# Padded value rows in DRAM, and keys, block rows and first weights requested later

## The chip, the cores and the metric

The kernel runs on one core of a Trainium2 chip. The metric is the device time of one execution in microseconds (us). Runs of this kernel before the change took 737.98, 738.64 and 740.18 us, median 738.64.

## The reference

Two parts follow each other. The first is an attention over 4 batches, 8 heads, 768 positions and head size 64. Each position sees its neighbours less than 16 away, and beside them 24 block summaries: of each block of 32 positions, the maximum of its keys and the mean of its values.

```python
k_sum = k.reshape(B, H, nb, block, D).max(axis=3)
v_sum = v.reshape(B, H, nb, block, D).mean(axis=3)
scores_l = scale * np.matmul(q, k.transpose(0, 1, 3, 2))        # masked to |i - j| < 16
scores_s = scale * np.einsum('bhsd,bhnd->bhsn', q, k_sum) + np.log(block)
a = softmax(concatenate([scores_l, scores_s]))
attn = np.matmul(a, concatenate([v, v_sum], axis=2))
```

The second is a mixture of 8 experts on the 3072 rows of the result (512 wide). A gate picks two experts for each row by noisy logits; each expert computes relu(x @ w1) @ w2 with a hidden size of 1024; the two results are added with softmax weights. All inputs are 32 bit.

## The kernel before, in words

**The attention** is cut into 24 steps of 128 queries, six to a batch. A step has two windows of 64 queries; for each, 94 keys and values and the 24 summaries make the 118 columns of its scores. The work of a step is spread over several turns of one loop over t: the turn computes the scores of step t + 2 (`scores`, L304), their row maximum on VectorE (`smax`, L311), transposes the probabilities of step t + 1 (L324), exponentiates those of step t + 2 on ScalarE (L318), multiplies the probabilities of step t with its values (`av`, L337, 32 matmuls), and normalizes step t - 1 (`norm`, L346 to L355). After that come the gate's own matmul (L378), for which the row is transposed (L366), and a store of the row, split into two 16-bit halves, to DRAM (`x_out`, L361, tile `xr` to `xd`).

**What the change touches** is how inputs reach the core. All plain loads are issued by the sync engine (SP), one after the other, and a load that must wait for its buffer holds up what is queued behind it.

- Keys (`load_k`, L102): two buffers `kb`, one for even and one for odd batches, each filled in halves of 384 positions. A margin of zero columns lies left and right of the keys; `kx_local` (L113) copies each window out of the buffer, and `k_piece` (L221) takes the block maxima on VectorE.
- Values of windows (`v_window`, L268, tile `vw`): for each window 96 rows of 520 numbers (8 heads, 64 values and a 1). A step's windows are asked for two steps ahead, when the buffers have been read. For batches 1 to 3 the first four windows also get the block sums (`v_rest`, L275).
- Block rows (`load_vb`, L135, landing in `htl`, `hth` and once in `stg`): the 32 values of a block of a head as one row, 96 rows at a time, in two halves of 16 values. VectorE adds the halves (`v_sum`, L229), GpSimd the rest (`v_sum2`, L234), and the sums are stored to DRAM (`v_sum_out`, L263) and read back by `v_rest`. Batch 0 has its sums from matmuls on tiles of 128 rows (`load_vn`, L140).
- Weights of expert 0, first half (`w_load`, L579, tile `stg`): four slices, each split into two 16-bit parts on ScalarE (`w_hi`, L587) and VectorE (`w_lo`, L596, `w1l`).

When each of these is placed is written out by hand: `at(t, f, ...)` puts a call into turn t of the loop, and the part behind the point says where in the turn (.5 ahead of `smax`, .1 to .3 ahead of `av`, .8 at the turn's end; a whole number just behind `av`, ahead of the turn's window loads). The lists W0 and WC place loads and splits of the weights, KL and KP loads and maxima of the keys (relative to the batch's six steps), VL loads and VS sums of the block rows.

Gates of whole groups of steps are worked out in the same way (`gate_a` to `gate_u`, from L398 on), most of it in small VectorE instructions; group 0 has the steps 0 to 4, group 1 the steps 5 to 9, group 2 the steps 10 to 12.

**The experts** follow. For each, rows are gathered by the gate's tables, transposed by DMA, and pass through the two products (`mm1`, L650, and `mm2`, L696 and L692), while the next expert's weights are loaded and split.

Of the kernel before, what the change touches and what calls it, by code (L numbers as in the profile page):

```python
# [17 lines left out]
B, H, S, D = 4, 8, 768, 64  # L18
BLK, WIN = 32, 16
NB = S // BLK  # L20
P = 128
# [8 lines left out]
W = 64 + 2 * (WIN - 1)  # L30
NK = W + NB
PAD = WIN - 1
KW = S + 2 * PAD + 2
VR = 96
VP = S + VR - 64
H0, CAP = 384, 816
# [4 lines left out]
CL = 1  # L41
SK = HP * NK
SW = 16 * (D + 1)
NCH = 7
R = 4096
RC = R // P
NS = 8 * NCH
GN = 5
# [10 lines left out]
def attn_moe(ctx, tc, qt, kt, vt, vb, wgn, noise, w1, w2, out):  # L59
    nc = tc.nc  # L60
# [27 lines left out]

    LAST = NCH - 1
    NL = CAP - LAST * P  # L90
    HWD = CAP + 64 - NL
    HT = [moe.tile([P, FC, HWD], F16, name=x) for x in ("hth", "htl")]
    KB, VW, KX = [], [], []
    for i in range(2):
        KB.append(keep.tile([P, HP, KW], F32, name=f"kb{i}"))
    for i in range(QN):
# [2 lines left out]
    QR = {}  # L99

    def load_k(b, j, n=1):
        nc.sync.dma_start(KB[b % 2][:, :, PAD + j * P:PAD + (j + n) * P], kt[b, :, :, j * P:(j + n) * P])  # L102

    def load_q(t):
        QR[t] = QT[t % QBUF]
# [2 lines left out]

    def kx_local(t):
        b, j = divmod(t, TS)  # L110
        k = KB[b % 2][:, :, j * P:j * P + 64 + W]
        for blk in range(2):
            (nc.vector if t < 2 else nc.gpsimd).tensor_copy(KX[t % QN][:, :, blk, NB:NK],  # L113
                                                            k[:, :, 64 * blk:64 * blk + W])
# [7 lines left out]
    def q_piece(t):  # L122
        kx_local(t)
        kx_sum(t)

    VB = {}

    def load_vb(u, i):
        n = 2 * u + i
        if n == 7:  # L130
            VB[u, i] = stage.tile([P, SW], F32, name="stg")
        else:
            n = n - 1 if n < 7 else (n - 8) % 6
            VB[u, i] = HT[n // 3].rearrange("p f n -> p (f n)").bitcast(F32)[:, SW * (n % 3):SW * (n % 3 + 1)]
        nc.sync.dma_start(VB[u, i][:96], vb[u * 96:(u + 1) * 96, SW * i:SW * i + SW])  # L135

    VN = [HT[0].rearrange("p f n -> p (f n)").bitcast(F32)[:, H * (D + 1) * j:H * (D + 1) * (j + 1)] for j in range(TS)]

    def load_vn(j):
        nc.sync.dma_start(VN[j].rearrange("p (h d) -> p h d", h=H), vt[0, PAD + j * P:PAD + (j + 1) * P])  # L140

    load_q(0)
    for j in range(0, TS, 2):
        load_k(0, j, 2)


    ji = HT[1].rearrange("p f n -> p (f n)").bitcast(I32)[:, SW:SW + P]
    nc.gpsimd.iota(ji, pattern=[[1, P]], base=0, channel_multiplier=-1)
# [10 lines left out]

    spare = [x.rearrange("p f n -> p (f n)").bitcast(F32)[:, 3 * SW:] for x in HT]  # L160
    dist, dist2 = [spare[1][:, W * i:W * i + W] for i in range(2)]
# [5 lines left out]
    for i in range(3):  # L167
# [8 lines left out]
                   allow_small_or_imprecise_dtypes=True)  # L176
    ind0 = HT[1].rearrange("p f n -> p (f n)").bitcast(F32)[:, 2 * SW:2 * SW + TS * NB].rearrange("p (t n) -> p t n", t=TS)
    nc.vector.tensor_scalar(ind0, ind, float(-BLK), None, op0=OP.is_gt)
# [8 lines left out]
    nc.gpsimd.iota(iotar, pattern=[[1, P]], base=0, channel_multiplier=0, allow_small_or_imprecise_dtypes=True)  # L187
    iotac = const.tile([P, E, NCH], F16, name="iotac")
    nc.gpsimd.iota(iotac, pattern=[[RC, E], [1, NCH]], base=0, channel_multiplier=0,
                   allow_small_or_imprecise_dtypes=True)  # L190
# [5 lines left out]
    wg32 = const.tile([P, DC, 16], F32, name="wg32")  # L196

    for x in KB:
        nc.gpsimd.memset(x[:, :, 0:PAD], 0.0)
        nc.gpsimd.memset(x[:, :, PAD + S:], 0.0)  # L200
    for i in range(8):
        VW.append(keep.tile([P, H, D + 1], F32, name=f"vw{i}"))
    late = []
# [1 line left out]
    for i in range(4):  # L205
        x = moe.tile([P, 2 * DM], F16, name=f"xg{i}")
# [10 lines left out]
    def k_piece(b, j, n=1):  # L217
        if j == 0:
            KM[b] = work.tile([P, HP, NB], F32, name="kmax")
        src = KB[b % 2][:, :, PAD + j * P:PAD + (j + n) * P]  # L220
        nc.vector.tensor_reduce(KM[b][:, :, 4 * j:4 * (j + n)],  # L221
                                src.rearrange("p h (n i) -> p h n i", i=BLK), axis=AX.X, op=OP.max)

# [41 lines left out]
    def v_window(blk):  # L265
        b, j = divmod(blk, 2 * TS)
        x = VW[(b % 2) * 4 + j % 4]
        nc.sync.dma_start(x[NB:NB + VR], vt[b, 64 * j:64 * j + VR])  # L268
        if j < 4 and b:
            v_rest(blk)  # L270
        return x

    def v_rest(blk):
        b, j = divmod(blk, 2 * TS)
        nc.sync.dma_start(VW[(b % 2) * 4 + j % 4][0:NB], vsd[b].rearrange("h n d -> n h d"))  # L275
# [3 lines left out]
    def v_load(t):  # L279
        VX[t] = [v_window(2 * t), v_window(2 * t + 1)]  # L280
# [180 lines left out]
    TB0 = const.tile([P, 3, 2], I32, name="tb0")  # L461
    TB = const.tile([P, E, NCH, 2], I32, name="tb")

# [105 lines left out]
    def w_alloc(e):  # L569
        pool = late[0] if e % 2 else wpool  # L570
        WT[e] = {n: pool.tile([P, 4, 1024], F16, name=f"{n}{e % 2}") for n in ("w1h", "w1l", "w2h", "w2l")}
# [50 lines left out]
    def x_gather(e, c, rows=N):  # L622
        if c == 0:
            XTE[e] = (late[0] if e % 2 else moe).tile([P, 2 * DC, CAP], F16, name="xte")
        n = min(P, CAP - c * P)
        x = XG[gi[0] % len(XG)]
        gi[0] += 1
        r = indirect(
            out=x[:n], out_offset=None, in_=xd[:rows],
            in_offset=bass.IndirectOffsetOnAxis(ap=tb_of(e, c)[:n, 0:1], axis=0),  # L630
            bounds_check=rows - 1, oob_is_err=False)
        XC[e, c] = x
        return r
# [87 lines left out]
    def at(t, f, *a):  # L721
        todo.setdefault(round(t, 3), []).append((f, a))
# [13 lines left out]
    for j in range(TS):  # L736
        load_vn(j)
# [4 lines left out]
    for j in range(4):  # L742
        k_piece(0, j)
    kx_local(0)
    for j in range(4, TS):
        k_piece(0, j)
# [3 lines left out]
    at(-0.8, v_first_out)  # L750

    w_alloc(0)
    W0 = [7, 11, 15, 18]
    WC = [10, 14, 17, 21]
    for i in range(4):
        at(W0[i], w_load, 0, i)
        at(WC[i] + 0.8, w_hi, 0, i)
        at(WC[i] + 1.8, w_lo, 0, i)
    VS = [(2, 3), (6, 7), (12, 14)]
    KP = [-3, -3, -2, -1, 1, 2]  # L760
    KP0 = [0, 1, 1, 2, 2, 2]
    KL = [-6, -6, -6, -3, -3, -3]
    VL = [(0, 1), (2, 2), (8, 9)]
    for b in range(B - 1):
        for j in range(TS):
            at(6 * b + KP[j] + 0.5 if b else KP0[j] + 0.5, k_piece, b + 1, j)
            if j % 3 == 0:
                at(6 * b + KL[j] if b else -1 + j // 3, load_k, b + 1, j, 3)
        for h in range(2):
            y = VS[b][h]  # L770
            for i in range(2):
                at(VL[b][h], load_vb, 2 * b + 2 + h, i)
            at(y + 0.5, v_sum, 2 * b + 2 + h)
            at(y + 0.1, v_sum2, 2 * b + 2 + h)
            at(y + 1, v_sum_out, 2 * b + 2 + h)
# [30 lines left out]
    for t in range(-2, NT):  # L806
        if t + QA < NT:
            load_q(t + QA)
        u = t + 3
# [22 lines left out]
        if u < NT and t >= 1:  # L832
            kx_local(u)
# [22 lines left out]
    for i in range(3):  # L856
        x = late[0].tile([P, DM], F32, name=f"prev{i}")
# [66 lines left out]
    assert not todo, todo  # L924
    for c in range(3, NCH):
        x_gather(0, c)
# [4 lines left out]
    k = 0  # L931
# [107 lines left out]
def layout(q, k, v, moe_w_gate, moe_w_noise, moe_noise, moe_w1, moe_w2):  # L1039
    import numpy as np  # L1040

    c = np.ascontiguousarray

    def heads(x):
        return c(x.reshape(B, HP, 2, S, D).transpose(0, 2, 4, 1, 3).reshape(B, 2 * D, HP, S))

    v1 = np.concatenate([v, np.ones((B, H, S, 1), v.dtype)], axis=3)
    vp = np.zeros((B, VP, H, D + 1), v.dtype)
    vp[:, PAD:PAD + S] = v1.transpose(0, 2, 1, 3)
    wgn = np.concatenate([moe_w_gate, moe_w_noise], axis=1).reshape(DC, P, 2 * E).transpose(1, 0, 2)  # L1050
    return {
        "qt": c(heads(q).reshape(B, 2 * D, HP, TS, P).transpose(0, 3, 1, 2, 4).reshape(B, TS, 2 * D, HP * P)),
        "kt": heads(k), "vt": vp,
        "vb": v1.reshape(B * H * NB, BLK * (D + 1)), "wgn": c(wgn),
        "noise": c(moe_noise.reshape(NT, P, E).transpose(1, 0, 2)), "w1": c(moe_w1), "w2": c(moe_w2),
    }

# [15 lines left out]
```

## Time and profile before

| | |
|---|---|
| median of three runs | 738.64 us |
| profiled execution | 741.86 us |
| its span, first to last instruction | 740.1 us |
| mean granted TensorE clock in it | 0.963 |
| TensorE busy | 694.0 us |
| VectorE busy | 323.2 us |
| ScalarE busy | 234.8 us |
| GpSimd busy | 283.1 us |
| moved by DMA | 126.21 MB |

The span is 1.8 us shorter than the time of the same execution; the rest lies around it. A row of the page that shows the span in 40 slices has one digit for each 18.5 us. The chain of waits gives a start, a length and what the time was spent on; a piece that begins with DMA is a wait for that transfer. A row of a stretch of time gives the stretch, its length, the busy time of the engines in the order TensorE, its weight load, VectorE, ScalarE, GpSimd with the number of instructions, the granted clock, the busy share of the 16 DMA engines and the rate in GB/s; asked for one line, only engines that run it appear. A row of waits gives the total, the count and the longest.

### The profile page before, as it was taken

Reading aid. Unit: us, or ns where it says so; the run is one execution under the profiler, and the core shown is the slowest. Engines: PE = TensorE matmul, PEld = TensorE weight load, DVE = VectorE, ACT = ScalarE, POOL = GpSimd, SP = SyncE. Lnnn points to the kernel's source line nnn. Section 1 sums busy time; section 2 is a strip of 40 time slices with the busy share of each in tenths; the row PEclk is TensorE's granted clock in tenths of the full one; section 3 lists DMA queues with packets and bytes.
Section 4 is the critical chain, followed back from the end, with each engine's and each line's share of the span. In section 5 each row is a group of like instructions: output and inputs, shape, how many; then the busy total and the mean of one; then the engine's idle time right before and its main releaser. Section 6 shows DMA issues by size and latency. Waiting matters only on the chain.

```text
span 740.1 us, 13612 instructions
## 1 busy us (share of the span) xinstructions
PE 694.0 (94%) x5330; PEld 409.2 (55%) x5330; DVE 323.2 (44%) x686; ACT 234.8 (32%) x523; POOL 283.1 (38%) x464
## 2 busy tenths in 40 slices
PE   7979897887989999999999999999999999999992
PEld 6667686765535555455446545554654555455441
DVE  6647868685934344234414431541353143412210
ACT  3568766771404044024203310430242033102100
POOL 2566556443040550553234243414432342340141
PEclk9999988985999999999999999999999999999997
DMA  9998987273269698569826941993497289511020
GB/s 284 283 281 249 278 230 215 92 186 122 88 156 364 207 276 195 151 179 222 235 84 162 198 169 65 192 224 131 112 214 180 86 169 163 159 47 38 23 80 33
DMA packets 105418, 126.21 MB, mean 171 GB/s; under 512 B 63701, under 2 KB 68445, under 8 KB 105344
## 3 DMA queue, kind: packets, MB, share of 16 engines
q1 hardware_dynamic: 93200, 88.96, 48.0%
q0 software_dynamic: 12144, 36.28, 18.1%
q8 instruction: 44, 0.72, 0.5%
q14 instruction: 30, 0.25, 0.1%
HBM read 88.14 MB, written 26.36 MB: 155 GB/s over the span
## 4 chain that ended last, share of the span: by engine, by line
PE 73%; DMA 11%; DVE 9%; SPq 1%; ACT 1%; POOL 1%; issue 1%; POOLq 0%; DVEq 0%
PE h L650 32%; PE pt L696 29%; PE pt L692 3%; DMA vw<-in_vt_dram 2%; PE o L337 2%; DMA htl<-in_vb_dram 2%; PE s L304 2%; DMA stg<-in_vb_dram 2%; PE pt L324 1%; PE o L378 1%; DMA stg<-in_w_dram 1%; DMA xd<-xr 1%; DMA xg<-xd,tb 1%; DVE w1l L596 1%; DVE w2l L596 1%
## 5 line engine op out<-in xcount | busy, mean ns | idle before, releaser
L650 PE MATMUL h<-xte,w1h 128*128 128x432 f16 (+1 forms) x1024 | 201.9, 338 | 3.6 <-DVE htl L655 2.9
L654 ACT ACTIVATE hth<-h 128x432 f16<-128x432 f32 (+1 forms) x128 | 63.7, 507 | 287.9 <-PE h L650 284.7
L86 POOL DMA_INDIRECT out_dram<-y,tb x48 | 53.4, 1113 | 244.7 <-DVE y L703 214.0
L650 PEld LDWEIGHTS <-w1h 128*128 128x128 f16 x1024 | 99.9, 98 | 81.1 <-issue 7.2
L696 PEld LDWEIGHTS <-hth 128*128 128x128 f16 x768 | 75.1, 98 | 91.8 <-issue 2.3
L655 DVE SCALAR_TENSOR_TENSOR htl<-h,hth 128x432 f16<-128x432 f32 (+1 forms) x128 | 73.2, 580 | 96.2 <-ACT hth L654 94.5
L650 PE MATMUL h<-xte,w1l 128*128 128x432 f16 (+1 forms) x512 | 109.9, 338 | 0.0
L703 DVE SCALAR_TENSOR_TENSOR y<-pt,tb,prev 128x512 f32<-128x512 f32 x42 | 31.5, 750 | 149.2 <-PE pt L696 149.2
L86 POOL DMA_INDIRECT xg<-xd,tb x56 | 58.9, 1052 | 95.9 <-DMA xte<-xg 59.7
L696 PE MATMUL pt<-w2l,hth 128*128 128x512 f16 x384 | 91.0, 379 | 1.5 <-DVE w2l L596 1.5
L696 PE MATMUL pt<-w2h,htl 128*128 128x512 f16 x384 | 90.7, 379 | 0.0
L696 PE MATMUL pt<-w2h,hth 128*128 128x512 f16 x384 | 90.7, 379 | 0.0
L650 PEld LDWEIGHTS <-w1l 128*128 128x128 f16 x512 | 50.3, 98 | 38.8 <-issue 0.9
L587 ACT ACTIVATE w2h<-stg 128x1024 f16<-128x1024 f32 x32 | 33.8, 1055 | 92.4 <-DMA stg<-in_w_dram 92.4
L696 PEld LDWEIGHTS <-htl 128*128 128x128 f16 x384 | 37.6, 98 | 45.3
L596 DVE SCALAR_TENSOR_TENSOR w2l<-stg,w2h 128x1024 f16<-128x1024 f32 x32 | 39.1, 1222 | 52.5 <-ACT w2h L587 51.8
L86 POOL DMA_INDIRECT prev<-out_dram,tb x42 | 46.9, 1116 | 10.9 <-issue 10.9
L318 ACT ACTIVATE p<-s,nm 128x118 f32<-128x118 f32 x192 | 50.5, 375 | 0.8
L358 POOL TENSOR_TENSOR xr<-x,xr 128x512 f16<-128x512 f32 x24 | 30.3, 1261 | 50.6 <-ACT xr L355 43.3
L596 DVE SCALAR_TENSOR_TENSOR w1l<-stg,w1h 128x1024 f16<-128x1024 f32 x32 | 41.7, 1302 | 15.3 <-ACT w1h L587 12.3
L337 PE MATMUL o<-vw,pts 118*64 118x65 f32 x768 | 34.9, 247 | 5.7 <-DMA vw<-in_vt_dram 5.6
L337 PEld LDWEIGHTS o<-vw,pts 118*64 118x64 f32 x768 | 30.3, 158 | 11.8 <-DMA vw<-in_vt_dram 8.3
(164 smaller groups left out, 641.9 us busy)
## 6 DMA issues: line engine op xcount, KB each, us to landing
stg<-in_w_dram SPq DMA_DIRECT2D x64, 512.0 KB
vw<-in_vt_dram SPq DMA_DIRECT2D x48, 195.0 KB
q<-in_qt_dram SPq DMA_DIRECT2D x24, 256.0 KB
xd<-xr SPq DMA_DIRECT2D x24, 256.0 KB
kb<-in_kt_dram SPq DMA_DIRECT2D x6, 768.0 KB
out_dram<-prev SPq DMA_DIRECT2D x6, 768.0 KB
htl<-in_vb_dram SPq DMA_DIRECT2D x6, 390.0 KB
hth<-in_vb_dram SPq DMA_DIRECT2D x5, 390.0 KB
```

Source lines behind the costliest of these rows:

```text
L86: return nc.gpsimd.indirect_dma_start(**kw)
L318: nc.scalar.activation(PE_[t][:, a, hp, :], SC[t][:, a, hp, :], AF.Exp, bias=NM[t][:, 1, a, hp:hp + 1], scale=0.125)
L337: nc.tensor.matmul(o[64 * blk:64 * blk + 64, h // 4, c:c + D + 1], PT[t][:NK, h % 2, h // 2, 64 * blk:64 * blk + 64], VX[t][blk][:NK, h, : ...
L358: nc.gpsimd.tensor_tensor(XR[t][:, DM:], X[t], XR[t][:, 0:DM], op=OP.subtract)
L587: nc.scalar.activation(WT[e][n + "h"][:, i % 4, :], SG[e, i], AF.Copy, scale=sc)
L596: nc.vector.scalar_tensor_tensor(lo, SG[e, i], sc, hi, op0=OP.mult, op1=OP.subtract)
L650: nc.tensor.matmul(ph[:, :n], w[wn][:, c, f * P:(f + 1) * P], x[:, xo + c, c0:c1], start=(k == 0), stop=(k == 11))
L654: nc.scalar.activation(hh[:, f, c0:c1], ph[:, :n], AF.Relu)
L655: nc.vector.scalar_tensor_tensor(hl[:, f, c0:c1], ph[:, :n], 0.0, hh[:, f, c0:c1], op0=OP.max, op1=OP.subtract)
L692: nc.tensor.matmul(py[64 * i:64 * i + 64, :HD], hx[:, f, c * P:c * P + 64], wv[:, f, HD * i:HD * i + HD], start=(k == 0), stop=(k == 23), ...
L696: nc.tensor.matmul(py, hx[:, f, c * P:c * P + P], wv[:, f, :], start=(k == 0), stop=(k == 23))
L703: nc.vector.scalar_tensor_tensor(y, py[:, :d], gw, pv[:, :d], op0=OP.mult, op1=OP.add)
```

## The change

Three things change.

1. In DRAM, the rows of the values (520 numbers, 2080 bytes) are padded to 576 numbers (2304 bytes), and the half rows of the block rows (1040 numbers, 4160 bytes) to 1088 (4352 bytes), so that each starts on a multiple of 256 bytes. The loads take the same numbers as before. The layout of the inputs is made ahead of the kernel.
2. The margin of the key buffer is 16 columns on each side; it was 15 on the left and 17 on the right. `kx_local` starts one column further right to read the same keys.
3. Requests move. Keys of batches 2 and 3: first half from six to three steps ahead of the batch before them, second half from three to one; the first four maxima come one step later too. Block rows of batch 2 from steps 2 and 2 to 4 and 5, those of batch 3 from 8 and 9 to 10 and 12. Weight slices from steps 7, 11, 15, 18 to 12, 14, 16, 18, their splits from 10, 14, 17, 21 to 15, 17, 19, 21. (A batch's block rows and keys are numbered by the batch that reads them.)

```diff
-KW = S + 2 * PAD + 2
+KO = 16
+KW = S + 2 * KO
+VC = H * (D + 1)
+VROW = 576
+VBROW = 1088
...
-        k = KB[b % 2][:, :, j * P:j * P + 64 + W]
+        k = KB[b % 2][:, :, KO - PAD + j * P:KO - PAD + j * P + 64 + W]
...
-        nc.sync.dma_start(VB[u, i][:96], vb[u * 96:(u + 1) * 96, SW * i:SW * i + SW])
+        nc.sync.dma_start(VB[u, i][:96], vb[u * 96:(u + 1) * 96, i, :SW])
...
-        nc.sync.dma_start(VN[j].rearrange("p (h d) -> p h d", h=H), vt[0, PAD + j * P:PAD + (j + 1) * P])
+        nc.sync.dma_start(VN[j], vt[0, PAD + j * P:PAD + (j + 1) * P, :VC])
...
-        nc.sync.dma_start(x[NB:NB + VR], vt[b, 64 * j:64 * j + VR])
+        nc.sync.dma_start(x[NB:NB + VR].rearrange("p h d -> p (h d)"), vt[b, 64 * j:64 * j + VR, :VC])
...
-    W0 = [7, 11, 15, 18]
-    WC = [10, 14, 17, 21]
+    W0 = [12, 14, 16, 18]
+    WC = [15, 17, 19, 21]
...
-    KP = [-3, -3, -2, -1, 1, 2]
+    KP = [-2, -2, -1, 0, 1, 2]
...
-    KL = [-6, -6, -6, -3, -3, -3]
-    VL = [(0, 1), (2, 2), (8, 9)]
+    KL = [-3, -3, -3, -1, -1, -1]
+    VL = [(0, 1), (4, 5), (10, 12)]
...
-    vp = np.zeros((B, VP, H, D + 1), v.dtype)
-    vp[:, PAD:PAD + S] = v1.transpose(0, 2, 1, 3)
+    vp = np.zeros((B, VP, VROW), v.dtype)
+    vp[:, PAD:PAD + S, :VC] = v1.transpose(0, 2, 1, 3).reshape(B, S, VC)
+    vb = np.zeros((B * H * NB, 2, VBROW), v.dtype)
+    vb[:, :, :SW] = v1.reshape(B * H * NB, 2, SW)
```

More of the change, by code (lines that the diff above doesn't have):

```diff
@@ L101, in load_k @@
     def load_k(b, j, n=1):
-        nc.sync.dma_start(KB[b % 2][:, :, PAD + j * P:PAD + (j + n) * P], kt[b, :, :, j * P:(j + n) * P])
+        nc.sync.dma_start(KB[b % 2][:, :, KO + j * P:KO + (j + n) * P], kt[b, :, :, j * P:(j + n) * P])
     def load_q(t):
@@ L198, in attn_moe @@
     for x in KB:
-        nc.gpsimd.memset(x[:, :, 0:PAD], 0.0)
-        nc.gpsimd.memset(x[:, :, PAD + S:], 0.0)
+        nc.gpsimd.memset(x[:, :, 0:KO], 0.0)
+        nc.gpsimd.memset(x[:, :, KO + S:], 0.0)
     for i in range(8):
@@ L219, in k_piece @@
             KM[b] = work.tile([P, HP, NB], F32, name="kmax")
-        src = KB[b % 2][:, :, PAD + j * P:PAD + (j + n) * P]
+        src = KB[b % 2][:, :, KO + j * P:KO + (j + n) * P]
         nc.vector.tensor_reduce(KM[b][:, :, 4 * j:4 * (j + n)],
@@ L1053, in layout @@
         "kt": heads(k), "vt": vp,
-        "vb": v1.reshape(B * H * NB, BLK * (D + 1)), "wgn": c(wgn),
+        "vb": vb, "wgn": c(wgn),
         "noise": c(moe_noise.reshape(NT, P, E).transpose(1, 0, 2)), "w1": c(moe_w1), "w2": c(moe_w2),
```

## The prediction, made before the changed kernel ran

> **What bounds the kernel now.** I read the slices of the page first (18.5 us each), then the chain that ended last, then one line's work in single stretches of time.
>
> ```profile
> PE   7979897887989999999999999999999999999992
> PEclk9999988985999999999999999999999999999997
> DMA  9998987273269698569826941993497289511020
> ```
>
> Up to 111 us (six slices) the 16 DMA engines are at least eight tenths busy and TensorE is not full. From the seventh slice the DMA engines have room, and from about 222 us TensorE is full to the end. The change moves transfers of the first six slices, so it is priced there. The chain says who is waited for:
>
> ```profile
> 27.33 11.89 DMA stg<-in_vb_dram
> 39.29 8.55 DMA htl<-in_vb_dram
> 47.90 7.58 DMA vw<-in_vt_dram
> ...
> 63.54 1.33 DVE hth L229
> ...
> 66.14 7.54 DMA xd<-xr
> 73.69 4.48 DMA htl<-in_vb_dram
> ...
> 82.37 9.71 DMA vw<-in_vt_dram
> 92.12 2.46 PE o L337 x32
> ...
> 100.05 1.08 PE o L337 x32
> ...
> 109.77 1.08 PE o L337 x32
> ...
> 119.90 2.53 DVE w1l L596
> ...
> 127.88 1.67 PE o L337 x32
> ```
>
> Six DMA pieces, 49.8 us together, stand in it between 27 and 92 us; after that come TensorE and VectorE. A step of the attention ends with the 32 matmuls of L337, so these rows are a clock for the steps: 100.05 is step 12 (counted from 0), 109.77 step 14, 127.88 step 16. Undisturbed, a step takes (109.77 - 100.05) / 2 = 4.86 us. The slow stretch:
>
> ```profile
> 28.90:99.80 70.90, 16.85 (x352) 14.22 (x352) 0.93 0.99 267
> ...
> 28.90:99.80 70.90, 61.80 (x964) 50.15 (x962) 49.30 (x116) 49.65 (x150) 46.96 (x64) 0.93 0.99 267
> ```
>
> In the first row, of L337 alone, 352 matmuls are 11 steps (1 to 11): 70.9 us, where 11 x 4.86 = 53.5 would do. The excess of 17.4 us is what this change can touch. In the second row TensorE is busy for 61.8 of it, so 9.1 us is plain idling; the rest is slower work, partly at a lower granted clock (0.93 here): after the wait that ends at 92.12, L337 takes 2.46 us, not 1.08. A wait removed takes such a tail with it.
>
> **Part 1: the padding.** It removes no byte and no transfer; each row of V windows (2080 B) and block rows (4160 B) now starts on a multiple of 256 B. It pays only if the starts are what makes these transfers slow. They are slow:
>
> ```profile
> 8.00:13.00 5.00, 2.78 (x58) 1.93 (x59) 4.32 (x11) 0.00 (x0) 0.94 (x2) 1.00 1.06 391
> 14.00:18.00 4.00, 4.00 (x31) 2.36 (x24) 1.14 (x1) 3.90 (x15) 0.00 (x0) 0.69 1.05 251
> 20.00:24.00 4.00, 4.00 (x50) 2.31 (x48) 1.95 (x4) 0.00 (x0) 1.19 (x3) 1.00 1.04 367
> 34.00:38.00 4.00, 3.46 (x70) 2.54 (x70) 3.05 (x6) 1.98 (x9) 3.84 (x5) 1.00 1.03 237
> ```
>
> ```profile
> 4.59 5.40 SPq L140 DMA_DIRECT2D hth<-in_vt_dram  x6
> 10.33 2.73 SPq L268 DMA_DIRECT2D vw<-in_vt_dram  x4
> ...
> 34.70 3.37 SPq L135 DMA_DIRECT2D hth<-in_vb_dram  x3
> ```
>
> The last column of the stretches is GB/s; the other rows are issues of the sync engine. The six L140 tiles, queued ahead of the windows, pass in the first stretch: rows of the same tensor, of the same 2080 B, at the same odd starts, but 128 rows each, and they run at 391 GB/s. Windows of 96 rows from that tensor follow (14 to 18: 251), block rows, again 96 rows, dominate the last (237). What separates 391 from 251 is the number of rows a transfer has, not where its rows start, so I take the padding's gain as 0; the other end is that all 96-row transfers rise to 367 (rival 1). Below nothing: a row pitch 11% wider (2304 for 2080) could slow reading by at most that 11%, 0.1 us per window of 195 KB.
>
> The Trainium skill (DMA: Bandwidth & Descriptors, "How a descriptor splits into AXI transactions") says a transfer that starts off a 256 B boundary also fetches the bytes from the boundary on; an estimate from it is 65 beats for an aligned 2080 B row and 68.5 on average now, 5% of each window. The 391 GB/s of the unaligned L140 rows shows no such 5%. The Trainium skill (SBUF — State Buffer, "Door 1: The DMA port swizzle") speaks against any gain: partitions 0 to 63 share eight of 16 ports, so 96 rows from 0 fill some ports twice as full as others, whatever the source's pitch; by it the block rows reach 391 x 96/128 = 293 GB/s at best, an estimate that lies on the same side as the 237.
>
> **Part 2: transfers asked for later.** Sizes and places:
>
> ```profile
> vw<-in_vt_dram SPq DMA_DIRECT2D x48, 195.0 KB
> kb<-in_kt_dram SPq DMA_DIRECT2D x6, 768.0 KB
> htl<-in_vb_dram SPq DMA_DIRECT2D x6, 390.0 KB
> stg<-in_w_dram SPq DMA_DIRECT2D x64, 512.0 KB
> q<-in_qt_dram SPq DMA_DIRECT2D x24, 256.0 KB
> xd<-xr SPq DMA_DIRECT2D x24, 256.0 KB
> ```
>
> ```profile
> 79.27 0.55 SPq L102 DMA_DIRECT2D kb<-in_kt_dram  x1
> 79.92 1.06 SPq L135 DMA_DIRECT2D hth<-in_vb_dram  x2
> 82.37 1.04 SPq L268 DMA_DIRECT2D vw<-in_vt_dram  x2
> ```
>
> The windows of step 11 are the 82.37 issue, and they landed at 92.1 because of what stood ahead in the same queue. Of that, the change puts behind them: one half of batch 3's keys (step 9 to 11; 786 kB at 367 GB/s = 2.1 us), four block-row loads (steps 8 and 9 to 10 and 12; 4 x 399 kB at 237 = 6.7 us) and one weight slice (step 7 to 12; 524 kB at 367 = 1.4 us). That is 10.2 us of queue time gone from before step 11. Within the stretch the rest is spread: batch 2's block rows go from one burst of four at step 2 (6.7 us) to two at step 4 and two at step 5, its keys from steps 0 and 3 to 3 and 5. A step's own transfers (two windows at 237, q and xd of 262 kB each at 367) take 1.7 + 1.4 = 3.1 us of 4.86, so a burst of four delays the next windows, and a pair (3.4 us) fits in two steps. I therefore expect the waits on windows to nearly vanish up to step 11, and TensorE to set the pace.
>
> What comes in their place, of the 17.4 us:
> - VectorE. The gate of the first batch ran under the 9.71 us wait and now stands in the open. The second batch's shows the price: steps 15 and 16 take 18.1 us (109.77 to 127.88), 8.4 over the pace, of which 2.5 is the weight split w1l at 119.90. Between 0 and the other 5.9, part of it a lower clock, I take the middle, 3 us. Four block sums of 1.33 us (L229, in the chain at 63.54) on steps that also reduce keys: 5.3 at most, 0 if idle time takes them; 2 us.
> - Keys. The key maximum (L221) sits in VectorE's order ahead of the scores' maximum; behind it wait exp, transposes and the next step. Its pieces come 1.5 steps (7.3 us) after their load, where there were 2.5 to 3.5. For batch 2's second half, issued behind two block-row loads, a window pair and q and xd (3.4 + 1.7 + 1.4 us, plus its own 2.1 = 8.6), the load ends 1.3 us too late, and I take 3 us with the clock's tail, which at 92.12 was 1.4 us on L337 alone. The other three are behind less: 0.
>
> ```profile
> DVE kmax L221 <- DMA kb<-in_kt_dram: 4.5, 3, 2.4
> SPq L102 <- POOL kx L113: 4.7, 1, 4.7
> ```
>
> Today's waits there are 4.5 us in all, longest 2.4: the lower end of that price is 0, the upper 4.6 a load (rival 3). The second row is a gain: SP stood 4.7 us in front of a key load whose buffer was still read, windows and q behind it; asked for three steps later, it finds the buffer free. At step 3 it stands behind the block-sum store (L263) in SP's order, as the second half did; what waits behind it (windows, q) waits no longer than now.
>
> So 17.4 - 3 - 2 - 3 = 9.4 us come out by step 12.
>
> **After step 12.** Block rows and a weight slice at step 12 (3.4 + 1.4 us on top of 3.1) make two steps' traffic in one: 1.5 us late once, between 0 (the seventh slice has room) and 4.8. The weight splits: the second moves from 15.8 to 18.8 in steps, away from the gate, and the third from 18.8 to 20.8.
>
> ```profile
> 119.82 2.61 DVE L596 SCALAR_TENSOR_TENSOR w1l<-stg,w1h 128x1024 f16<-128x1024 f32 x1
> ...
> 129.60 0.17 DVE L346 TENSOR_SCALAR r<-o 128x8 f32<-128x8 f32 x1 [2.27 <-PE o L337]
> ...
> 141.64 1.22 DVE L596 SCALAR_TENSOR_TENSOR w1l<-stg,w1h 128x1024 f16<-128x1024 f32 x1
> ...
> 155.20 0.15 DVE L346 TENSOR_SCALAR r<-o 128x8 f32<-128x8 f32 x1
> ```
>
> The 2.5 us at 119.9 leave the chain. The first split now falls into the 2.27 us in which VectorE idled before 129.60: 0. The third falls right ahead of 155.20, where VectorE had no idle time: 1.2 us. Net 1.3 gained. The other edits (16 columns of margin for 15, reads of keys shifted by one column) change no size: 0, with the copies of keys on GpSimd off the chain. What follows the attention is the same work in the same order and starts earlier by the same amount.
>
> Sum: 9.4 - 1.5 + 1.3 = 9.2 us gained. The profiled execution took 741.86 us (span 740.1), so 732.7; the median of the runs is 738.64, 3.2 below it, so I forecast **729.5 us**; its own range is 724 to 735, from the 5 us of gate and sums being nothing or double.
>
> **The rivals.**
> 1. The padding does lift the 96-row transfers to 367 GB/s. Against it stands the 391 of unaligned rows; for it, that nothing in the page excludes an effect of the pitch across 96 rows. A window pair falls from 1.7 to 1.1 us and a block pair from 3.4 to 2.2; then the keys are in time (3 us) and step 12's load fits (1.5): 725.
> 2. What the DMA gives back is taken by VectorE, which is 49.3 us busy in the 70.9 and then has 15% less time: every step with a gate or a block sum runs at VectorE's pace. If the exposed work is 13 us, not 5, the result is 738, no change.
> 3. Slower: the key loads. All four have 1.5 steps of lead. If each is late by 4.5 us (two block pairs and a window pair queued ahead: 6.7 + 1.7 + 1.4 + 2.1 = 11.9 against 7.3), VectorE stands four times, 18 us for the 3 priced: 744.5. It decides from 3 us a load on.
>
> **How the numbers follow.** Chances: forecast 0.57, rival 1 0.18, rival 2 0.13, rival 3 0.12. 0.3% (2.2 us) is about what a measurement of this kernel tells from no change. Faster than 736.4: the forecast and rival 1, 0.75; same 0.13; slower 0.12. The range reaches from 722 (rival 1 and no exposed gate) to 738.5, over most of rival 2, and leaves out rival 3.
>
> **What would show it.** Right: the 32 matmuls of step 12 start near 90 us, not 100; no DMA piece over 5 us in the chain between 30 and 90; GB/s with block rows in flight stays near 240. Rival 1 shows as 350 or more there. Rival 3 shows as VectorE waiting on keys for over 10 us. The forecast fails if step 12 is early and step 23 is not: then the gates, not the transfers, set the stage's end.

## The result and the profile after

The changed kernel is slower: 745.37 us (743.62 to 748.81) where the kernel before took 738.31 beside it, a ratio of 1.010 [1.0057, 1.0143]. Its profiled execution took 745.14 us, its span is 743.3 (740.1 before), its mean granted clock 0.958 (0.963). The lines of the changed kernel are four further down: L337 is now L341, L221 is L225, L102 is L106, L135 is L139, L311 is L315.

Three rows of the slices of the changed kernel (18.6 us each):

```profile
PE   7988888986899999999999999999999999999992
...
PEclk9997978896999999999999999999999999999997
DMA  8998887543449799459925962962399278211020
```

The granted clock is lower than before in the fourth slice (7 for 9) and the sixth (7 for 8); the DMA engines have room from the seventh slice on, as before. The stretch of steps 1 to 11, L341 alone and then all lines (columns as before):

```profile
28.90:103.90 75.00, 15.24 (x352) 13.55 (x352) 0.86 0.92 250
...
28.90:103.90 75.00, 64.64 (x964) 52.56 (x963) 44.59 (x113) 48.69 (x147) 44.39 (x62) 0.86 0.92 250
```

The same 352 matmuls take 75.0 us, where they took 70.9: the excess over 53.5 grew from 17.4 to 21.5 us. TensorE idles for 10.4 (9.1 before), the granted clock is 0.86 (0.93), and the DMA engines are 0.92 busy (0.99): they are no longer what everybody waits for. The chain of the changed kernel:

```profile
44.82 5.10 DMA vsd<-htl
52.10 7.91 DMA kb<-in_kt_dram
...
68.70 1.93 PE o L341 x32
...
75.62 1.08 PE o L341 x32
...
80.55 1.14 PE o L341 x32
83.47 8.54 DMA htl<-in_vb_dram
92.03 7.43 DMA kb<-in_kt_dram
99.52 3.96 DMA hth<-in_vb_dram
```

Not one of the waits on windows (vw<-in_vt_dram) of before is left up to 92 us; loads of keys and block rows and a store of block sums stand in their place. Waits between 24 and 112 us, the stretch of all moved loads of batches 2 and 3:

```profile
ACT nm L319 <- DVE nm L315: 16.4, 6, 4.0
DVE kmax L225 <- DMA kb<-in_kt_dram: 9.4, 4, 3.3
```

The key maximum waits 9.4 us (2.4 before, one wait). Where it does, the step is long. The ends of the 32 matmuls of a step in the trace (one execution of each kernel), in us, with the length of the step behind the bar:

| step | before | changed | padding only (e1) | keys only (e5) | keys in between (e6) | 
|---|---|---|---|---|---|
| 4 | 50.2 / 7.2 | 46.7 / 4.8 | 51.9 / 9.5 | 48.6 / 5.1 | 47.2 / 4.8 |
| 5 | 56.7 / 6.4 | 56.0 / 9.2 | 58.6 / 6.6 | 62.6 / 14.0 | 52.6 / 5.4 |
| 7 | 66.8 / 5.1 | 70.6 / 9.7 | 68.1 / 4.8 | 73.8 / 5.8 | 66.1 / 7.3 |
| 10 | 84.7 / 6.3 | 86.4 / 4.8 | 85.3 / 5.3 | 89.7 / 4.8 | 81.5 / 5.1 |
| 11 | 94.6 / 9.9 | 100.4 / 14.0 | 95.6 / 10.3 | 104.9 / 15.2 | 90.4 / 9.0 |
| 12 | 101.1 / 6.6 | 105.4 / 5.0 | 101.0 / 5.4 | 109.7 / 4.8 | 95.5 / 5.0 |
| 23 | 175.8 / 9.8 | 181.4 / 11.5 | 175.4 / 11.2 | 186.8 / 11.0 | 171.5 / 11.4 |

At step 4 the changed kernel was 3.5 us ahead. It lost that and more in steps 5, 7 and 11. The first of the three, in the trace of the changed kernel in order of time (in brackets the idle time before, and what ended it):

```profile
46.41 1.28 DVE L225 TENSOR_REDUCE kmax<-kb 128x16 f32<-128x512 f32 x2 [3.09 <-DMA kb<-in_kt_dram]
...
47.61 1.13 DVE L315 TENSOR_REDUCE nm<-s 128x8 f32<-128x944 f32 x1
...
48.77 0.21 ACT L319 ACTIVATE nm<-nm 128x8 f32<-128x8 f32 x1 [3.70 <-DVE nm L315]
...
49.42 1.07 PE L328 MATMUL pt<-ident,p 128*118 128x128 f32 x4 [1.27 <-ACT p L322]
...
51.66 0.65 PE L328 MATMUL pt<-ident,p 128*118 128x128 f32 x4 [1.16 <-ACT xt L372]
...
53.98 2.00 PE L341 MATMUL o<-vw,pts 118*64 118x65 f32 x32
```

VectorE stands 3.09 us in front of the key maximum, with the scores' maximum (L315) behind it in its order; ScalarE then waits 3.70 for that, TensorE 1.27 and 1.16 for ScalarE, and the 32 matmuls of step 5 take 2.00 us, where those of step 4 took 1.16. TensorE alone in stretches of 1 us (stretch, length, busy, granted clock, DMA share, GB/s):

```profile
47.00:48.00 1.00, 1.00 (x34) 1.00 1.06 364
48.00:49.00 1.00, 0.16 (x8) 1.00 1.14 322
49.00:50.00 1.00, 0.57 (x3) 1.00 0.97 206
50.00:51.00 1.00, 0.49 (x2) 1.00 1.02 217
51.00:52.00 1.00, 0.34 (x3) 1.00 1.00 206
...
53.00:54.00 1.00, 1.00 (x7) 0.50 0.89 231
...
55.00:56.00 1.00, 1.00 (x21) 0.50 1.03 376
56.00:57.00 1.00, 1.00 (x18) 0.81 1.16 404
```

From 48 to 52 TensorE is busy for 1.56 of 4 us. From 53 to 56 it is always busy, at half the clock. So with a wait of 3.1 us on VectorE the step is 9.2 - 4.86 = 4.3 us over the pace. The other two, on VectorE:

```profile
60.03 0.69 DVE L225 TENSOR_REDUCE kmax<-kb 128x16 f32<-128x512 f32 x1 [2.72 <-DMA kb<-in_kt_dram]
...
86.39 1.28 DVE L225 TENSOR_REDUCE kmax<-kb 128x16 f32<-128x512 f32 x2 [3.29 <-DMA kb<-in_kt_dram]
```

Step 7, behind the 2.72, is 4.8 us over the pace; VectorE also has a block sum there (L233, 1.23 us at 60.63), between the key maximum and the scores' maximum. Step 11, behind the 3.29, also has the first gate; it took 14.0 us.

### The profile page after: what moved, and what is told of

The parts are those of the page before. It is cut to its first block, busy times and chain, and to the rows that moved or that the text cites. A ratio compares the mean times of both kernels' runs of the same rounds, so it can differ in the third digit from the quotient of the medians.

```text
span 743.3 us, 13614 instructions
## 1 busy us (share of the span) xinstructions
PE 694.9 (93%) x5330; PEld 410.6 (55%) x5330; DVE 321.3 (43%) x686; ACT 235.7 (32%) x523; POOL 280.1 (38%) x464
## 4 chain that ended last, share of the span: by engine, by line
PE 73%; DVE 8%; DMA 7%; POOL 4%; SPq 3%; issue 2%; ACT 1%; POOLq 0%; DVEq 0%
PE pt L700 31%; PE h L654 31%; DMA kb<-in_kt_dram 3%; PE pt L696 3%; PE o L341 2%; PE o L382 1%; SPq L641 1%; PE s L308 1%; DMA htl<-in_vb_dram 1%; PE pt L328 1%; POOL htl L238 1%; POOL out_dram L90 1%; PE pt L370 1%; POOL kx L117 1%; DVE w2l L600 1%
## 5 line engine op out<-in xcount | busy, mean ns | idle before, releaser
L90 POOL DMA_INDIRECT prev<-out_dram,tb x42 | 44.4, 1057 | 10.8 <-issue 10.6
L362 POOL TENSOR_TENSOR xr<-x,xr 128x512 f16<-128x512 f32 x24 | 28.7, 1195 | 49.5 <-ACT xr L359 36.7
L328 PE MATMUL pt<-ident,p 128*118 128x128 f32 x192 | 30.4, 292 | 10.3 <-ACT xt L372 6.2
L382 PE MATMUL o<-wg,xt 128*128 128x16 f32 x176 | 24.6, 273 | 14.8 <-DVE lg L390 8.2
```

Source lines behind the costliest of these rows:

```text
L90: return nc.gpsimd.indirect_dma_start(**kw)
L328: nc.tensor.transpose(pt[:NK, hp, :], PE_[t][:, a, hp, :], ident)
L362: nc.gpsimd.tensor_tensor(XR[t][:, DM:], X[t], XR[t][:, 0:DM], op=OP.subtract)
L382: nc.tensor.matmul(o[:, 0, GO:GO + 16], XT[t][:, c, :], wg32[:, c, :], start=(c == 0), stop=(c == DC - 1), skip_group_check=True)
```

## The experiments

The theory after the result: the key loads, each asked for too late, make VectorE stand, and that alone turns the gain of the other two moves into a loss. Rivals: the padding slows the loads; the later block rows or weights collide with something; VectorE's own work, now uncovered, sets the time whatever the loads do. All ratios are to the kernel before, run beside on the same chip. It took 741.5 to 743.7 us there, while the expectations given in us go by the 738.3 of the result, so they are to be read as ratios to that.

### One part at a time

e1 takes the changed kernel and puts the old places back, so that only the layout (padding and margin) is left:

```diff
-    W0 = [12, 14, 16, 18]
-    WC = [15, 17, 19, 21]
+    W0 = [7, 11, 15, 18]
+    WC = [10, 14, 17, 21]
...
-    KP = [-2, -2, -1, 0, 1, 2]
+    KP = [-3, -3, -2, -1, 1, 2]
...
-    KL = [-3, -3, -3, -1, -1, -1]
-    VL = [(0, 1), (4, 5), (10, 12)]
+    KL = [-6, -6, -6, -3, -3, -3]
+    VL = [(0, 1), (2, 2), (8, 9)]
```

> The changed layout (padded value and block rows, 16 columns of margin) with the order of requests of the kernel before. Theory (the late keys cost the time, the padding nothing): the same as before, within 2 us of it, and the rate with block rows in flight stays near 240 GB/s. Rival (the padding itself costs): 743 to 747 us.

e4 is the reverse, the kernel before with the changed W0, WC, KP, KL and VL and the old layout:

> The layout of the kernel before with the changed order of requests. Theory (late keys): as slow as the changed kernel, 743 to 747 us. Rival (the padding costs): as before, 737 to 740 us. Rival (the padding helps and hides part of the loss): 748 us or more.

The other three are the kernel before with one move each. e5 has the keys:

```diff
-    KP = [-3, -3, -2, -1, 1, 2]
+    KP = [-2, -2, -1, 0, 1, 2]
...
-    KL = [-6, -6, -6, -3, -3, -3]
+    KL = [-3, -3, -3, -1, -1, -1]
```

> The kernel before, with nothing changed but the requests of keys and the steps of their maxima (KL, KP as in the changed kernel). Theory (late keys are the whole loss, and the other moves gain): slower than before by 1 to 2%, with VectorE waiting on keys for 8 us or more, since the block rows still stand in bursts. Rival (late keys hurt only together with the moved block rows queued ahead of them): within 0.4% of before.

e8 has the block rows, `VL = [(0, 1), (4, 5), (10, 12)]`:

> The kernel before with nothing changed but the requests of block rows (VL as in the changed kernel). Theory (spreading the burst of four takes waits on windows away): 0.3 to 1% faster than before, step 5 ends 3 us earlier. Rival (block rows come too late for their sums): the same or slower, with VectorE waiting on block rows.

e9 has the weights, `W0 = [12, 14, 16, 18]` and `WC = [15, 17, 19, 21]`:

> The kernel before with nothing changed but the requests and splits of expert 0's first four weight slices (W0, WC as in the changed kernel). Theory (the parts add up: keys alone +1.7%, block rows alone -0.4%, keys of before with the other two moved -0.7%): about 0.997 of before. Rival (the splits delay VectorE and ScalarE late in the attention): 1.000 or more.

| kernel | median us | ratio to before |
|---|---|---|
| e1, layout only | 742.56 | 0.9985 [0.9958, 1.0012] |
| e4, all moves, old layout | 749.16 | 1.0056 [1.0022, 1.0090] |
| e5, keys only | 753.79 | 1.0172 [1.0135, 1.0210] |
| e8, block rows only | 739.75 | 0.9959 [0.9931, 0.9988] |
| e9, weights only | 740.54 | 0.9967 [0.9936, 0.9998] |

The sign of the change is that of the keys alone: 1.7% slower, while block rows and weights each gain 0.3 to 0.4%. The four parts add up to -0.15 + 1.72 - 0.41 - 0.33 = +0.83%, inside the interval of the whole (+0.57 to +1.43). The layout is no different from nothing, alone (e1) or by the overlap of e4 with the changed kernel. The interval of e9 barely leaves out 1. The waits of e5 (line numbers of the kernel before), over the whole run:

```profile
DVE kmax L221 <- DMA kb<-in_kt_dram: 14.5, 6, 7.0
```

With the block rows still in bursts of four, one key load makes VectorE stand for 7.0 us, and step 5 is 14.0 us long (table above). In e8, over the whole run, a wait on windows (8.3 us before) and the wait on keys (4.5):

```profile
PEld o L337 <- DMA vw<-in_vt_dram: 5.2, 9, 1.4
...
DVE kmax L221 <- DMA kb<-in_kt_dram: 1.8, 3, 0.7
```

The later block rows alone shorten both, and step 12 ends at 97.3 us, not 101.1. This is the part that worked, though step 5 ends only 1.0 us earlier (55.7 for 56.7) where I had expected 3.

### Keys in time, by three ways

All three are the changed kernel with other places of the keys. e2 puts loads and maxima back (`KL = [-6, -6, -6, -3, -3, -3]`, `KP = [-3, -3, -2, -1, 1, 2]`), e3 leaves the loads late and takes the maxima one turn later still (`KP = [-1, -1, 0, 1, 1, 2]`), e6 has the maxima of e3 and asks for the keys in between (`KL = [-4, -4, -4, -3, -3, -3]`).

> The changed kernel with keys and their maxima (KL, KP) where they were before. Theory (late keys): VectorE's waits on keys fall from 9.4 us to about 3, steps 5, 7 and 11 lose 3 to 5 us each, and the time falls by 9 to 14 us below the changed kernel, to 731 to 736 us. Rival (the early key load blocks the sync engine again and windows are waited for as before): 738 to 741 us. Rival (weights and gates set the end): 743 to 746 us.

> The changed kernel with every load where it is now, but the first four key maxima one step later still (KP = -1, -1, 0, 1, 1, 2). It takes VectorE's waits away without moving a transfer. Theory (the wait in VectorE's order is the cost, not the place of the load): waits on keys under 2 us, 731 to 737 us. Rival (late transfers cost in another way, on GpSimd's copies or on the windows): 742 us or more.

> The changed kernel with keys asked for in between (KL = -4 and -3: steps 2 and 3, 8 and 9, ahead of the block rows of steps 4, 5, 10, 12) and the first four maxima one step later still, as in e3. Theory (what is left of the stalls are late keys and late read-backs of block sums behind them): no wait of VectorE on keys, and 3 to 6 us below e3, 0.985 to 0.990 of the kernel before. Rival (with the key waits gone VectorE and the gates set the pace): the same as e3, 0.993 of before within 0.003.

| kernel | median us | ratio to before |
|---|---|---|
| e2, keys back | 739.56 | 0.9932 [0.9900, 0.9964] |
| e3, maxima later | 738.01 | 0.9931 [0.9903, 0.9960] |
| e6, loads in between | 737.53 | 0.9940 [0.9913, 0.9967] |

Each way brings the kernel from 1.0% slower to 0.6 or 0.7% faster than before. The waits of the key maximum over the whole run, 11.2 us in the changed kernel, in e2 and in e3:

```profile
DVE kmax L225 <- DMA kb<-in_kt_dram: 2.5, 2, 1.7
```

```profile
DVE kmax L225 <- DMA kb<-in_kt_dram: 3.8, 3, 2.0
```

Between 24 and 112 us, 0.8 us of it is left in e2 and 2.0 in e3, for 9.4. That settles the cause of the loss; e3 does it without moving one transfer, only what waits for it. But the three are alike, and e6, which I had expected to come in clearly below e3, does not. The longest delay left in e3 is a late transfer of its own, in its chain:

```profile
57.38 8.23 DMA vw<-vsd
65.75 1.97 PE o L341 x30
```

The block sums, read back from DRAM, hold step 7 there (10.4 us long). (Behind it, from 81 to 96 us, the chain of e3 also has a load of block rows of 8.24 us and one of keys of 6.75.) In e6 the longest wait on read-back sums is 0.8 us. The stretch of steps 1 to 11 in e6, L341 alone, and its waits from 24 to 96 us:

```profile
29.30:94.30 65.00, 14.63 (x353) 12.66 (x353) 0.97 1.01 273
```

```profile
ACT nm L319 <- DVE nm L315: 11.5, 8, 2.7
...
PEld o L341 <- DMA vw<-in_vt_dram: 3.6, 5, 1.0
...
PE o L341 <- DMA vw<-vsd: 2.5, 4, 0.8
...
DVE kmax L225 <- DMA kb<-in_kt_dram: 0.4, 1, 0.4
```

65.0 us for 70.9 before, so 5.9 us of the 17.4 came out, and 11.5 stay although nobody waits for keys (0.4). Its step 11, the longest with 9.0 us:

```profile
80.00 1.47 PE L341 MATMUL o<-vw,pts 118*64 118x65 f32 x32
...
81.42 1.55 DVE L494 TENSOR_TENSOR lh<-iotar,rf 128x640 f16<-128x640 f16 x2
...
83.25 0.80 DVE L504 TENSOR_TENSOR oc<-iotac,qf 128x280 f16<-128x280 f16 x2
...
83.97 0.16 DVE L350 TENSOR_SCALAR r<-o 128x8 f32<-128x8 f32 x1
...
88.44 2.00 PE L341 MATMUL o<-vw,pts 118*64 118x65 f32 x32
```

The 32 matmuls of step 10 end at 81.47; their normalization (L350) begins at 83.97, behind the gate's work in VectorE's order. TensorE runs dry and its next 32 matmuls take 2.00 us. No transfer takes part in it.

### Quicker transfers

The block rows can be loaded 128 at a time instead of 96, with 32 rows that nobody uses (133 KB more for each load; the array in DRAM is 32 rows longer):

```diff
-        nc.sync.dma_start(VB[u, i][:96], vb[u * 96:(u + 1) * 96, i, :SW])
+        nc.sync.dma_start(VB[u, i], vb[u * 96:u * 96 + P, i, :SW])
```

e7 is e3 with it, e10 is e6 with it, e12 is e2 with it.

> e3 with block rows loaded 128 at a time where 96 are used (a third more bytes; the 32 further rows land in partitions that nobody reads). Theory (transfers of 96 rows are slow for their number of rows, not for where rows start): the rate with block rows in flight rises from about 240 to 330 GB/s or more, a packet of 4160 B falls from 270 to about 165 ns, and the load takes no longer than before; the time is that of e3 within 0.4%. Rival (something else slows these reads, such as long strides in DRAM): the rate stays near 240 and the loads take a third longer, 3 us or more above e3.

> e6 with block rows loaded 128 at a time. Theory (VectorE and the gates set the pace once the keys are in time, so quicker transfers bring little): 0.989 to 0.994 of before. Rival (the transfers still set the pace): under 0.988.

> e2 (keys and maxima where they were before, block rows and weights moved) with block rows loaded 128 at a time. Theory: 0.989 to 0.993 of before, level with e10, since neither waits for keys. Rival (the key load of step 0, which stops the sync engine for its buffer, costs): 0.994 or more.

First the rate (the last column, GB/s). The changed kernel, with the six L140 tiles in flight, whose 128 rows now start on multiples of 256 bytes, and then with block rows; below it e3 and e7, with block rows:

```profile
8.00:13.00 5.00, 2.57 (x45) 1.34 (x42) 4.38 (x11) 0.00 (x0) 0.92 (x2) 0.90 1.05 391
...
26.00:36.00 10.00, 9.30 (x166) 7.26 (x162) 8.25 (x13) 7.22 (x22) 7.96 (x10) 1.00 1.04 241
```

```profile
30.00:32.00 2.00, 2.00 (x42) 1.70 (x41) 1.93 (x5) 2.00 (x7) 2.00 (x3) 1.00 1.08 230
48.00:50.00 2.00, 2.00 (x42) 1.71 (x41) 1.87 (x5) 1.67 (x5) 0.23 (x1) 1.00 1.03 257
```

```profile
30.00:32.00 2.00, 2.00 (x42) 1.66 (x41) 1.93 (x5) 2.00 (x7) 2.00 (x3) 1.00 1.01 404
48.00:50.00 2.00, 2.00 (x42) 1.68 (x41) 1.86 (x6) 1.67 (x5) 0.19 (x1) 1.00 1.03 413
```

Same padding and same places in the order: 230 and 257 GB/s with 96 rows, 404 and 413 with 128. A quarter of the bytes of a load of 128 rows is not used, so 404 is about 300 GB/s of what is needed. By the packets in the traces, a row of 4160 bytes takes 268 ns (median) in e3 and 161 in e7, as expected. The padding changed nothing: 241 GB/s in the changed kernel and 237 before, each in a stretch with block rows in flight; 260 ns for a row of 4160 bytes before and 261 in e1; and 391 GB/s for the L140 tiles, aligned now and unaligned before. Then the time:

| kernel | median us | ratio to before | the same with 96 rows |
|---|---|---|---|
| e7 | 738.16 | 0.9947 [0.9923, 0.9971] | e3, 0.9931 |
| e10 | 735.85 | 0.9929 [0.9893, 0.9964] | e6, 0.9940 |
| e12 | 736.63 | 0.9936 [0.9904, 0.9968] | e2, 0.9932 |

Step 12 ends at 98.9 us in e7 and 99.1 in e3, at 95.3 in e10 and 95.5 in e6, at 95.6 in e12 and 97.8 in e2. e10 and e12 did not go lower than their twins by anything that these runs can tell. e12 lies between the two expectations for it (0.993 and less, 0.994 and more). With the keys in time, a quicker load of block rows brings nothing that these runs show. The windows, which are also loads of 96 rows, were not made quicker in any run.

### Less work on VectorE

e11 is e6 without the first addition of the block sums on VectorE (`v_sum`; lines behind it are one lower than in e6):

```diff
-        nc.vector.tensor_add(x, x, z)
```

> e6 without VectorE's addition of the two halves of block rows (left out: half of the values' block sums of batches 1 to 3; six instructions of 1.3 us). Theory (VectorE's work is what stands in the open where the waits on transfers were): steps 3, 7 and 12 lose 1 to 2 us each, 3 to 6 us below e6. Rival (the additions lie beside other work): the same as e6 within 2 us.

734.84 us, 0.9865 [0.9803, 0.9927]; the interval touches that of e6 (0.9940 [0.9913, 0.9967]), so from the time alone the half per cent between them is likely, not shown. The trace is clearer. The waits of ScalarE on the scores' maximum from 24 to 96 us in e11:

```profile
ACT nm L318 <- DVE nm L314: 3.0, 5, 1.0
```

3.0 us for 11.5 in e6, and step 3, where a sum stands ahead of the scores' maximum, takes 5.2 us for 7.0. Step 11 with its gate takes 8.8 (9.0): the gate stays. The rest of the expectation failed: step 7 takes 7.2 us (7.3 in e6) and step 12 takes 5.5 (5.0), while step 13, which I had not named, takes 4.8 (7.3). Steps 5 to 8 take 24.6 us together (24.3), so the additions are not what is lost there.

## Why the prediction was wrong

The forecast of 9.2 us gained turned into 3.2 us lost between the spans of the two profiled executions, and 7.1 between the medians. Steps 1 to 11 were to take 53.5 + 8 = 61.5 us; they took 75.0. Term by term, over the pace of 4.86 us:

| term | predicted | measured |
|---|---|---|
| keys | 3 | 3.8 (step 5, 9.2 - 5.4) + 2.4 (step 7, 9.7 - 7.3) + 5.0 (step 11, 14.0 - 9.0), each against the same step of e6 = 11.2 |
| the first gate | 3 | 4.1 (step 11 of e6, 9.0 - 4.86; no run leaves the gate out) |
| block sums | 2 | 2.0 (step 3, 6.9 - 4.86; e11 takes 1.8 off the 7.0 of e6) |
| windows | 0 | 0, no wait on them up to step 11 |
| not priced | 0 | 0.5 and 2.4 (what steps 5 and 7 keep over the pace in e6, where nobody waits for keys) + 1.2 (step 8) = 4.1, which I can't put down to one wait |

The sum of the last column is 21.4, the excess 21.5. **The step that failed is the price of the keys**: "the load ends 1.3 us too late, and I take 3 us", for one load, and "The other three are behind less: 0". The runs show 11.2 us in its place, and the whole stretch is 10.0 us shorter in e6 than in the changed kernel (65.0 for 75.0). That is 8.2 of the 13.5 us by which the stretch was missed. (Against the pace instead of e6 the three steps would give 4.3 + 4.8 + 5.0 = 14.1, but 2.4 us of step 7 stay in e6 without a wait on keys.) Two readings in it were wrong. The issues of SP in the changed kernel:

```profile
39.61 0.33 SPq L267 DMA_DIRECT2D vsd<-hth  x1
40.03 0.56 SPq L106 DMA_DIRECT2D kb<-in_kt_dram  x1
...
52.10 0.56 SPq L106 DMA_DIRECT2D kb<-in_kt_dram  x1
...
78.53 0.57 SPq L106 DMA_DIRECT2D kb<-in_kt_dram  x1
```

- The lead. I took "1.5 steps (7.3 us)" from the numbers in the lists. VectorE was ready for the keys at 43.32 (46.41 - 3.09), 57.31 and 83.10 us, that is 3.3, 5.2 and 4.6 us behind the issues. A place in the list is a place in an engine's order, not a time: VectorE reaches the point of turn 4.5 right behind the normalization that follows the matmuls of step 3 (42.0 us), and SP reaches turn 3 late, here directly behind the store of the block sums (39.61). I had named that store, and priced only what waits behind it for other tiles.
- The load. I took 2.1 us for 786 kB at 367 GB/s and looked for queue time only ahead of one load. From issue to use the three took 6.4, 7.9 and 7.9 us, and the fourth 7.43 by the chain. By the packets in the trace, the keys begin to move 1.4 to 2.5 us behind the issue and then take 3.9 to 5.0 us, with other loads in flight. The trace of the kernel before has it too: the last packets of its four loads of half a batch, issued at 24.49, 44.82, 62.97 and 79.27 us, end 6.6 to 8.1 us behind the issue. Its chain shows only a smaller one, the second of the three loads of batch 0 (512 KB) at the start:

```profile
1.94 6.20 DMA kb<-in_kt_dram
```

With a load of 6.4 to 7.9 us and a lead of 3.3 to 5.2, each of the three is late by about 3 us. **Rival 3** had this: all four loads late, VectorE standing, "It decides from 3 us a load on", 744.5 us; the measured time is 745.4. Its sign, over 10 us of waiting on keys, came (11.2 over the whole run). In detail it was three waits and not four (the fourth is 0.3 us), and shorter: 9.1 us together, for 18. They cost 11.2 by the table, and other terms were off too, so it is luck that 744.5 and 745.4 lie so close. I gave it 0.12 and ended the range at 738.5, short of it.

**Rival 2** holds for a part of what is left. With the keys in time the change would have brought 0.6%, not the 1.2% of the forecast: e6 took 5.9 us out of the stretch, where the forecast without its 3 us for keys is 17.4 - 5 = 12.4. The exposed work of VectorE, 6.2 us there (4.1 and, in step 3, 2.1) instead of 5, is 1.2 of the difference. The rest is in steps 5 to 8 of e6 (5.4, 6.2, 7.3 and 5.4 us, 4.9 over the pace) and 0.4 in others. What these four steps lose stays open: neither e11 (24.6 us together) nor the quicker block rows of e10 (24.1) shortens them by more than 0.2 of the 24.3 in e6. 6.1 us of waits on windows and read-back sums remain in e6, 0.3 in the changed kernel, so the expectation of "the waits on windows to nearly vanish" seems to hold there because it stands still elsewhere meanwhile; no run shows this by itself. The exposed work is 6.2 us and not the 13 of rival 2. (Its "15% less time" is 13%, 9.4 of 70.9 us.)

Other points:

- **The padding at 0** was right (e1: 0.9985 [0.9958, 1.0012]), and so was the reason, as far as e7 shows it for block rows: their rate goes by the number of rows in a transfer (or by the partitions that these fill, which e7 changes with it). Rival 1 fell, since the rate stayed at 241; that a rate of 404 for the block rows brought no time (e7) speaks against its gain too, without excluding one from quicker windows. The 391 GB/s of unaligned rows, which I took as a sign against an effect of the starts, became one only with the 391 of the aligned rows beside it. The Trainium skill (DMA: Bandwidth & Descriptors, "How a descriptor splits into AXI transactions") gives an estimate of 5% on each window; no rate and no time here shows it. By the Trainium skill (SBUF — State Buffer, "Door 1: The DMA port swizzle") 96 rows lose against 128, which agrees; the 293 GB/s estimated from it are more than the 230 to 257 measured.
- **After step 12** I had -1.5 and +1.3. From step 12 to 23 the changed kernel takes 76.0 us (74.7 before), 1.3 lost instead of 0.2. e9, the weights alone, takes 73.4 there, which bears out the +1.3 in one execution. Behind step 23 the changed kernel takes 561.9 us for 564.3, which I had at 0; the same part takes 561.9 to 567.2 in the traces of the twelve experiments, so these 2.4 us are not shown to be a gain.
- **The signs.** Step 12 was to start near 90 us and started at 104.2. In e6 it starts at 94.3. No piece of DMA over 5 us was to be left in the chain from 30 to 90 us; three begin there, of 5.1 to 8.5 us, and a fourth at 92.

No version beats the others for sure: e2, e3, e6, e7, e10 and e12 lie between 0.993 and 0.995, so about 1.6% under the changed kernel (0.994 / 1.010). The smallest edit of the changed kernel that gets there is e3's, one list.

## What to carry to other kernels

A load that is moved closer to its use is priced by two times in the trace: from its issue to its landing under the traffic of that stage, and from the moment its queue reaches the issue to the moment the consumer's engine is ready; places in a list give neither. Look at what stands behind the consumer in its engine's order: a wait on a side job (here the maximum of the next batch's keys) holds up the main line, and can cost more than it lasts once TensorE runs dry (3.3 us cost 5.0 in step 11). When transfers stop being the bound, look for what the next engine does in that stretch: of the 11.5 us over the pace that stay with the keys in time, 6.2 are by the trace VectorE's own gate and sums.

## What the hardware showed

- Loads of 4160-byte rows ran at 230 to 257 GB/s with 96 rows and at 404 to 413 with 128, in the same stretches of e3 and e7.
- TensorE's granted clock fell to 0.50 for about 3.4 us, from 53.0 us on in the changed kernel, after 4 us (48 to 52) in which it was busy for 1.56 us, with no single gap longer than 1.3 us. The Trainium skill (TensorE: Matmul & The Clock Gate, "Why this matters for your kernels") warns of idle gaps above about 3 us; here the clock fell behind two short ones close together, of 1.27 and 1.16 us.
